# Diagonal bonus terms of the attention: eight scaled ACT copies instead of one POOL multiplication

## The chip, the cores and the metric

The kernel runs on one core of a Trainium2 chip. It is one launch that does an attention with a decaying state, a gated feed-forward block and a mixture of eight experts. The metric is the device time of the core in microseconds (us), lower is better; it is measured in several runs, and one further execution is recorded by the hardware profiler. Engines: TensorE (PE, with its weight loads PEld), VectorE (DVE), ScalarE (ACT), GpSimd (POOL), and SyncE (SP), which issues the DMA transfers.

## The reference, cut to what matters

The attention goes through 768 steps for 4 batches and 8 heads of 48 channels. The part that the change touches is the term with `u`, a bonus for the current step: summed over the channels it is the scalar `sum_d r*k*u` of a head and a position, which multiplies that position's `v`.

```python
for t in range(S):
    kt, vt, rt, wt = (k[:, :, t], v[:, :, t], r[:, :, t], w[:, :, t])
    cur = np.einsum('bhd,bhe->bhde', u[None] * kt, vt)
    y[:, :, t] = np.einsum('bhd,bhde->bhe', rt, state + cur)
    state = wt[:, :, :, None] * state + np.einsum('bhd,bhe->bhde', kt, vt)
...
a = x @ w1; b = x @ w2; h = a * b @ w3; x = h @ w_out
```

Behind it come a gate that is normalised eight times over rows and columns, and eight experts of the form `max(x @ w1[e], 0) @ w2[e]`.

## The kernel before

The attention is done in 24 units of 128 positions (four batches, six units each), all eight heads of a unit together. A unit goes through four phases, one in each step of a loop over steps `s`; the unit is `s // 4`, the phase `s % 4`:

- phase 0: `stage_a0` of the next unit. PE transposes the decays into `trw` and the keys into `trk`; ACT copies `trw` out (L278, tile `w33`, shown as `w<-trw`). Then f_rk multiplies r, k and u on POOL (L305, L306, tile `rk`). Somewhat later in the same step `stage_a1` has PE transpose r into `trr`.
- phase 1: `stage_b`: PE makes the scores `sc`, ACT copies out the transposed keys (`kn`), DVE masks the scores into `A` (L376) and adds the diagonal terms `ec` to it (L377).
- phases 2 and 3: `stage_c1` and `stage_c2`: PE multiplies `A` with the values (`yt`), DVE updates the states, ACT copies the result into `xraw` (L436, L438).

`stage_a0` also queues eight small operations, of which two are taken in each step: two scans on DVE (L309, L312), small products, the scaled keys and r (`Kt`, `Rt`, DVE and POOL) and, as the last, `f_cc`, so that f_cc is reached in phase 3, ahead of the next step's `stage_a0`. f_cc sums `rk` over the channels on DVE (tile `cc`, 128 positions x 8 heads, L344), and makes from it the diagonal terms `ec` (128 x 2 x 4 x 64, L345).

```python
pw = ps.tile([P, NP, P], F32, tag="tr", bufs=2, name="trw")
...
pk = ps.tile([P, NP, P], F32, tag="tr", bufs=2, name="trk")
...
pr = ps.tile([P, NP, P], F32, tag="tr", bufs=2, name="trr")
...
aux.extend([f_scan_f, f_scan_g, f_small, f_ks, f_rp, f_kx, f_rx, f_cc])
```

The three transposes share a PSUM tag with two buffers. The order of each engine's work is the order in which the program emits it; nothing reorders it.

The feed-forward block runs in the same steps, for blocks of three units. From s = 15 on the steps repeat in twelves: eight MoE steps (`moe_a`: nine matmuls into `pa`, ACT copies them to `asb`, L475; `moe_b`: nine into `pb`, DVE multiplies with `asb` to `gs`, L488, ACT rounds to `gh`, L489, POOL keeps the rest `gl`, L490) and four x2 steps (18 matmuls into `po`, ACT copies them out, L518). In an MoE step of phase 0 the order is `stage_a0`, `moe_a`, one queued operation, `stage_a1`, `moe_b`, one queued operation. In the first 30 steps the weights are also unpacked from 64-bit numbers (`cv`, `wo`: ACT L160, DVE L165 to L167; `w1h`, `w2h` ACT L213; `w1l`, `w2l` POOL L214), and a product of two weight matrices is made (`w34`).

After the attention, from about 530 us on, PE works through the experts (`zp`, `yp`).

Of the kernel before, what the change touches and what calls it, by code (L numbers as in the profile page):

```python
# [14 lines left out]
AF = mybir.ActivationFunctionType  # L15
ALU = mybir.AluOpType
# [15 lines left out]
def tile_rwkv_moe_sinkhorn_moe(  # L32
# [16 lines left out]
    nc = tc.nc  # L49
    B, H, S, D = r.shape  # L50
# [3 lines left out]
    P = 128  # L54
    DP = 64
    NP = H // 2
# [18 lines left out]
    def mm(o, lhsT, rhs, start, stop, pos=None, tr=False, skip=False):  # L75
        kw = {}
        if skip:
            kw["skip_group_check"] = True
        if pos is not None:
            kw["tile_position"] = pos  # L80
        if tr:
            kw["is_transpose"] = True
        nc.tensor.matmul(o, lhsT, rhs, start=start, stop=stop, **kw)  # L83
# [4 lines left out]
    eye = const.tile([P, DP], F32, name="eye")  # L88
# [184 lines left out]
    def stage_a0(n):  # L273
        wt, kt = nat["w", n % 2], nat["k", n % 2]
        pw = ps.tile([P, NP, P], F32, tag="tr", bufs=2, name="trw")
        for p in range(NP):
            mm(pw[:, p, :], wt[:, 2 * p:2 * p + 2, :].rearrange("p a d -> p (a d)"), ident, True, True, tr=True)
        nc.scalar.activation(W33B[:, :, 0:32], pw.rearrange("p a (b s) -> p (a b) s", s=32), AF.Copy)  # L278
        pk = ps.tile([P, NP, P], F32, tag="tr", bufs=2, name="trk")
        for p in range(NP):  # L280
            mm(pk[:, p, :], kt[:, 2 * p:2 * p + 2, :].rearrange("p a d -> p (a d)"), ident, True, True, tr=True)
        d = st[n] = {"pk": pk}
        Ft = att.tile([P, 528], F32, tag="F", name="Ft")
        Gt = att.tile([P, 529], F32, tag="G", name="Gt")
        M = att.tile([P, 2, 2, 8], F32, tag="M", bufs=2, name="Mt")
        T12 = att.tile([P, NP, 2], F32, tag="T12", bufs=2, name="T12")
        Rt = att.tile([P, 34 * 32], F32, tag="R", bufs=2, name="Rt")
        rk = att.tile([P, H, D], F32, tag="rk", name="rk")
        cc = att.tile([P, H], F32, tag="cc", bufs=2, name="cc")
        d.update(R=Rt, T12=T12, v=nat["v", n % 2])  # L290
        F3 = Ft.rearrange("p (b s) -> p b s", s=33)
        Fv = F3.rearrange("p (c b) s -> p b c s", b=2)[:, :, :, 0:32]
        Tv = F3.rearrange("p (c b) s -> p b c s", b=2)[:, :, :, 32]
        Gv = Gt[:, 1:529].rearrange("p (c b s) -> p b c s", b=2, s=33)[:, :, :, 1:33]

        def diag(t):
            return t.rearrange("p (g a s) -> p g a s", g=2, s=32)[:, :, 0:16:2, :]

        def off(t):
            return t[:, 32:32 * 31].rearrange("p (g a s) -> p g a s", g=2, s=32)[:, :, 0:15:2, :]  # L300

        nrt, nkt = nat["r", n % 2], nat["k", n % 2]

        def f_rk():
            nc.gpsimd.tensor_tensor(rk, nrt[:, :, 0:D], nkt[:, :, 0:D], op=ALU.mult)  # L305
            nc.gpsimd.tensor_tensor(rk, rk, ub, op=ALU.mult)  # L306

        def f_scan_f():
            nc.vector.tensor_tensor_scan(Ft, w33[:, 0:528], d1[:, 0:528], 0.0, op0=ALU.mult, op1=ALU.add)  # L309

        def f_scan_g():
            nc.vector.tensor_tensor_scan(Gt[:, 2:529][:, ::-1], w33[:, 2:529][:, ::-1], d1[:, 2:529][:, ::-1],  # L312
                                         0.0, op0=ALU.mult, op1=ALU.add)

        def f_small():
            nc.vector.tensor_copy(M[:, :, 1, :], Tv)
            nc.vector.reciprocal(M[:, :, 0, :], M[:, :, 1, :])
            nc.vector.tensor_tensor(T12.rearrange("p a b -> p (a b)"), M[:, 0, 1, :], M[:, 1, 1, :], op=ALU.mult)

        def f_ks():  # L320
            Kt = att.tile([P, 34 * 32], F32, tag="K", bufs=1, name="Kt")
            d["K"] = Kt
            kv = pk.rearrange("p a (c b s) -> p b (a c) s", b=2, s=32)
            nc.vector.tensor_tensor(diag(Kt), kv, Gv, op=ALU.mult)

        def f_kx():
            Kt = d["K"]
            m_ = M[:, 1, :, :].unsqueeze(3).to_broadcast([P, 2, 8, 32])
            for g in range(2):
                nc.gpsimd.tensor_tensor(off(Kt)[:, g], diag(Kt)[:, 1 - g], m_[:, g], op=ALU.mult)  # L330

        def f_rp():
            rv = d["pr"].rearrange("p a (c b s) -> p b (a c) s", b=2, s=32)
            nc.vector.tensor_tensor(off(Rt)[:, ::-1], rv, Fv, op=ALU.mult)

        def f_rx():
            m_ = M[:, 0, :, :].unsqueeze(3).to_broadcast([P, 2, 8, 32])
            for g in range(2):
                nc.gpsimd.tensor_tensor(diag(Rt)[:, g], off(Rt)[:, 1 - g], m_[:, g], op=ALU.mult)

        def f_cc():
            ec = att.tile([P, 2, NP, DP], F32, tag="ec", bufs=1, name="ec")
            d["ec"] = ec
            nc.vector.tensor_reduce(cc, rk, axis=AX.X, op=ALU.add)  # L344
            nc.gpsimd.tensor_tensor(  # L345
                ec, eye.unsqueeze(1).unsqueeze(1).to_broadcast([P, 2, NP, DP]),
                cc.rearrange("p (a h) -> p h a", h=2).unsqueeze(3).to_broadcast([P, 2, NP, DP]), op=ALU.mult)

        f_rk()
        aux.extend([f_scan_f, f_scan_g, f_small, f_ks, f_rp, f_kx, f_rx, f_cc])  # L350
# [725 lines left out]
```

## Time and profile before

| what | value |
|---|---|
| median of 3 runs | 2104.77 us (2103.47 to 2104.82) |
| profiled execution, its own time | 2102.65 us |
| span of its instructions | 2100.9 us |
| mean granted clock of PE | 0.991 |
| PE busy | 2045.1 us |
| DVE, ACT, POOL busy | 1143.0, 552.4, 489.2 us |

The span goes from the first instruction to the last; the rest of the execution's time lies around it. Busy time leaves out waiting. The granted clock is the share of full speed (2.4 GHz) that PE had.

### The profile page before, as it was taken

To read this page: it belongs to the slowest core of one execution; us is meant where nothing else is said; L and a number is where in the kernel's file an instruction comes from. 1 tells how busy PE (TensorE), PEld (TensorE's weight loads), DVE (VectorE), ACT (ScalarE), POOL (GpSimd) and SP (SyncE) were. 2 spreads that over 40 slices of the span, in tenths; PEclk is the share of its full clock that TensorE was granted. 3 is DMA by queue.
4 is the path that set the end of the run, shared out by engine and by line. 5 is a ranking of instruction groups with operands and counts; after the bars stand their busy time and mean duration, and the time that the engine had idled before them with its cause. 6 is when DMAs were issued, how large, how long until landed. Compare 5 with 4: busy or idle time off the path is not lost.

```text
span 2100.9 us, 37959 instructions
## 1 busy us (share of the span) xinstructions
PE 2045.1 (97%) x16427; PEld 1991.1 (95%) x16427; DVE 1143.0 (54%) x1792; ACT 552.4 (26%) x956; POOL 489.2 (23%) x487
## 2 busy tenths in 40 slices
PE   5879999999999999999999999999999999999999
PEld 4569999999999999999999999999999999999999
DVE  8786666661575464454455545544545454445444
ACT  3443333333322221231123112211321131123111
POOL 4475555555513210030003001200300030011000
PEclk8999999999999999999999999999999999999999
DMA  7652222211412222132124122321321232213220
GB/s 229 134 102 49 50 50 50 49 25 48 180 46 91 104 93 91 56 128 104 46 91 146 50 91 69 128 91 46 135 98 54 91 111 86 91 61 117 100 86 31
DMA packets 145287, 183.67 MB, mean 87 GB/s; under 512 B 105120, under 2 KB 133856, under 8 KB 137952
## 3 DMA queue, kind: packets, MB, share of 16 engines
q1 hardware_dynamic: 145120, 181.25, 26.9%
q8 instruction: 129, 2.11, 0.4%
q14 instruction: 38, 0.31, 0.1%
HBM read 161.17 MB, written 18.87 MB: 86 GB/s over the span
## 4 chain that ended last, share of the span: by engine, by line
PE 92%; DVE 4%; DMA 1%; issue 1%; POOL 1%; ACT 1%; SPq 0%; DVEq 0%; ACTq 0%; POOLq 0%
PE yp L83 38%; PE zp L83 35%; PE po L83 5%; PE pa L83 5%; PE pb L83 4%; PE yt L83 1%; DVE cv L166 1%; DMA nat_w<-in_w_dram 1%; PE sc L83 1%; PE trn L83 1%; PE w34ps L83 1%; DVE cv L167 0%; PE trw L83 0%; PE up L83 0%; PE trk L83 0%
## 5 line engine op out<-in xcount | busy, mean ns | idle before, releaser
L83 PE MATMUL zp<-xc,w1h 128*128 128x256 f32 x4224 | 783.2, 280 | 7.7 <-DVE hl L848 6.7
L83 PEld LDWEIGHTS zp<-xc,w1h 128*128 128x128 f32 x4224 | 692.1, 189 | 9.5 <-issue 7.8
L83 PE MATMUL zp<-xc,w1l 128*128 128x256 f32 x2112 | 594.8, 282 | 0.0
L83 PE MATMUL yp<-w2h,hh 128*128 128x384 f32 x1536 | 517.6, 337 | 0.0
L83 PE MATMUL yp<-w2l,hh 128*128 128x384 f32 x1536 | 516.5, 336 | 0.1
L83 PE MATMUL yp<-w2h,hl 128*128 128x384 f32 x1536 | 516.2, 336 | 0.0
L83 PEld LDWEIGHTS zp<-xc,w1l 128*128 128x128 f32 x2112 | 398.7, 189 | 0.0
L844 ACT ACTIVATE hh<-cc 128x512 fp32r<-128x512 f32 x288 | 182.2, 633 | 814.5 <-DVE cc L851 814.5
L652 POOL TENSOR_TENSOR w1l<-w1raw,w1h 128x768 fp32r<-128x768 f32 x32 | 59.2, 1850 | 1086.1 <-ACT w1h L651 1086.1
L83 PEld LDWEIGHTS yp<-w2h,hh 128*128 128x128 f32 x1536 | 289.8, 189 | 0.1
L83 PEld LDWEIGHTS yp<-w2l,hh 128*128 128x128 f32 x1536 | 288.9, 188 | 0.4 <-DVE w2l L666 0.4
L83 PEld LDWEIGHTS yp<-w2h,hl 128*128 128x128 f32 x1536 | 288.4, 188 | 0.0
L851 DVE TENSOR_TENSOR cc<-u,zp 128x512 f32<-128x512 f32 x192 | 131.9, 687 | 270.5 <-PE zp L83 270.5
L851 DVE TENSOR_TENSOR u<-t,zp 128x512 f32<-128x512 f32 x192 | 131.9, 687 | 193.7 <-PE zp L83 162.8
L848 DVE SCALAR_TENSOR_TENSOR hl<-cc,hh 128x512 fp32r<-128x512 f32 x288 | 199.0, 691 | 7.6 <-ACT hh L844 7.4
L959 DVE SCALAR_TENSOR_TENSOR acc<-yp,Pm,acc 128x384 f32<-128x384 f32 x168 | 103.4, 616 | 117.0 <-PE yp L83 116.8
L844 ACT ACTIVATE hh<-zp 128x512 fp32r<-128x512 f32 x96 | 57.5, 599 | 253.0 <-PE zp L83 253.0
L848 DVE SCALAR_TENSOR_TENSOR hl<-zp,hh 128x512 fp32r<-128x512 f32 x96 | 65.8, 686 | 72.8 <-ACT hh L844 72.8
L490 POOL TENSOR_TENSOR gl<-gs,gh 128x384 fp32r<-128x384 f32 x64 | 72.1, 1127 | 109.2 <-ACT gh L489 109.1
L851 DVE TENSOR_TENSOR vv<-u,zp 128x512 f32<-128x512 f32 x96 | 66.1, 688 | 49.2 <-PE zp L83 48.4
L488 DVE TENSOR_TENSOR gs<-pb,asb 128x384 f32<-128x384 f32 x64 | 35.5, 555 | 103.1 <-PE pb L83 65.0
L867 ACT ACTIVATE t<-zp 128x512 f32<-128x512 f32 x96 | 57.4, 598 | 124.4 <-PE zp L83 124.4
(151 smaller groups left out, 2370.3 us busy)
## 6 DMA issues: line engine op xcount, KB each, us to landing
xc<-xd SPq DMA_DIRECT2D x42, 2304.0 KB, 8.7
xd<-xc SPq DMA_DIRECT2D x6, 2304.0 KB, 7.0
w2raw<-in_moe_w_dram SPq DMA_DIRECT2D x32, 384.0 KB, 3.5
raw<-in_moe_w_dram SPq DMA_DIRECT2D x8, 1024.0 KB, 5.0
w1raw<-in_moe_w_dram SPq DMA_DIRECT2D x32, 256.0 KB, 2.8
nat_w<-in_w_dram SPq DMA_DIRECT2D x24, 192.0 KB, 3.7
nat_k<-in_k_dram SPq DMA_DIRECT2D x24, 192.0 KB, 3.5
nat_r<-in_r_dram SPq DMA_DIRECT2D x24, 192.0 KB, 3.7
```

The costliest lines, as they stand in the source:

```text
L83: nc.tensor.matmul(o, lhsT, rhs, start=start, stop=stop, **kw)
L166: nc.vector.scalar_tensor_tensor(cu, lw, 29, cu, op0=ALU.logical_shift_right, op1=ALU.bitwise_or)
L488: nc.vector.tensor_tensor(gs, pb, asb, op=ALU.mult)
L490: nc.gpsimd.tensor_tensor(gl[:, f, :], gs, gh[:, f, :].bitcast(F32), op=ALU.subtract)
L652: nc.gpsimd.tensor_tensor(lo[:, d0:d0 + n, :], src, hi[:, d0:d0 + n, :].bitcast(F32), op=ALU.subtract)
L844: nc.scalar.activation(hh, src, AF.Relu)
L848: nc.vector.scalar_tensor_tensor(hl, src, 0.0, hh.bitcast(F32), op0=ALU.max, op1=ALU.subtract)
L851: nc.vector.tensor_tensor(o, a, b_, op=ALU.add)
L867: nc.scalar.activation(t1, b1, AF.Copy)
L959: nc.vector.scalar_tensor_tensor(dst, ya[t], Pm[:, tt, e:e + 1], dst, op0=ALU.mult, op1=ALU.add)
```

## The change

The sum on DVE stays. Instead of one POOL multiplication of the identity (repeated over the heads) with the sums (repeated over the columns), ACT copies the 128x64 identity once for each head, with that head's sums as a scale per partition, into that head's part of `ec`. The eight copies are emitted at the place where the POOL operation was.

```diff
             nc.vector.tensor_reduce(cc, rk, axis=AX.X, op=ALU.add)
-            nc.gpsimd.tensor_tensor(
-                ec, eye.unsqueeze(1).unsqueeze(1).to_broadcast([P, 2, NP, DP]),
-                cc.rearrange("p (a h) -> p h a", h=2).unsqueeze(3).to_broadcast([P, 2, NP, DP]), op=ALU.mult)
+            for h in range(H):
+                nc.scalar.activation(ec[:, h % 2, h // 2, :], eye, AF.Copy, scale=cc[:, h:h + 1])
```

## Rows read from the trace of the kernel before

**Rows 1.** Busy time by stretch: stretch, length, engines, PEclk, DMA share, GB/s.
```profile
0.00:100.00 100.00, 67.95 (x597) 45.43 (x598) 81.38 (x107) 38.11 (x60) 48.11 (x47) 0.88 0.72 187
100.00:200.00 100.00, 87.55 (x1003) 76.25 (x1002) 76.38 (x108) 37.15 (x71) 63.91 (x50) 0.95 0.44 79
...
400.00:500.00 100.00, 100.00 (x1195) 94.38 (x1194) 50.94 (x92) 33.49 (x74) 50.96 (x52) 1.00 0.17 42
```

**Rows 2.** Tile ec: duration in ns (min/median/max), first and last start.
```profile
L345 POOL TENSOR_TENSOR ec<-eye,cc x24: 1049/1885/2027, 13.4 to 468.7; 128x512 f32<-128x512 f32 x24
```

**Rows 3.** The chain that ended last, at 151 us: start, length, what.
```profile
151.19 1.72 POOL ec L345
...
156.52 2.72 POOL w2l L214
```

**Rows 4.** Timeline around 159 us, DVE and PE: start, length, [idle before].
```profile
158.38 1.40 DVE L377 TENSOR_TENSOR At<-At,ec 128x512 f32<-128x512 f32 x1
...
159.29 0.44 PE L83 MATMUL pb<-xh,w2l 128*128 128x384 f32 x1 [2.05 <-POOL w2l L214]
...
160.71 0.69 PE L83 MATMUL yt<-At,nat_v 64*64 64x64 f32 x32
```

**Rows 5.** Timeline of DVE and POOL in the first 60 us.
```profile
37.53 2.03 POOL L345 TENSOR_TENSOR ec<-eye,cc 128x512 f32<-128x512 f32 x1
38.68 1.95 DVE L167 SCALAR_TENSOR_TENSOR cv<-raw,cv 128x1024 uint32<-128x1024 uint32 x1
...
59.81 1.52 DVE L167 SCALAR_TENSOR_TENSOR cv<-raw,cv 128x1024 uint32<-128x1024 uint32 x1
```

**Rows 6.** ACT's groups by form: busy us, mean ns of one; Pm: ns.
```profile
L489 ACT ACTIVATE gh<-gs 128x384 fp32r<-128x384 f32 x64 | 33.6, 525 | 113.9 <-DVE gs L488 113.9
L213 ACT ACTIVATE w1h<-cv 128x768 fp32r<-128x768 f32 x4 | 3.4, 842 | 11.8 <-DVE cv L167 11.8
L990 ACT ACTIVATE Pm<-L,nmx x1: 444/444/444, 563.4 to 563.4; 128x192 f32<-128x192 f32 x1
```

**Rows 7.** Timeline of ACT and PE in an x2 step of phase 0.
```profile
427.92 0.53 ACT L489 ACTIVATE gh<-gs 128x384 fp32r<-128x384 f32 x1 [1.70 <-DVE gs L488]
428.35 0.36 ACT L436 ACTIVATE xraw<-yt 128x256 f32<-128x256 f32 x1
428.74 0.78 ACT L438 ACTIVATE xraw<-yt 64x256 f32<-64x256 f32 x2
431.62 0.60 ACT L278 ACTIVATE w<-trw 128x512 f32<-128x512 f32 x1 [2.09 <-PE trw L83]
...
434.98 0.60 PE L83 MATMUL trr<-ident,nat_r 128*128 128x128 f32 x4
```

**Rows 8.** Who waited for line L278 (ACT's w): us, times.
```profile
PEld trr L83: 0.8, 3
```

**Rows 9.** Timeline, MoE step of phase 0, first kind, and ACT's w at 449.50.
```profile
396.49 0.54 DVE L344 TENSOR_REDUCE cc<-rk 128x8 f32<-128x384 f32 x1
397.10 0.58 ACT L278 ACTIVATE w<-trw 128x512 f32<-128x512 f32 x1
398.19 0.60 PE L83 MATMUL trr<-ident,nat_r 128*128 128x128 f32 x4
...
449.50 0.58 ACT L278 ACTIVATE w<-trw 128x512 f32<-128x512 f32 x1
```

**Rows 10.** Timeline of an MoE step of phase 0, second kind.
```profile
415.14 0.58 ACT L278 ACTIVATE w<-trw 128x512 f32<-128x512 f32 x1
...
416.26 0.60 PE L83 MATMUL trr<-ident,nat_r 128*128 128x128 f32 x4
```

**Rows 11.** A pause of PE, and busy time with PEclk behind two pauses.
```profile
605.49 0.77 PE L83 MATMUL zp<-xc,w1h 128*128 128x256 f32 x2 [3.26 <-DVE hl L848]
...
159.20:164.00 4.80, 4.71 (x84) 4.40 (x85) 4.52 (x11) 0.79 (x2) 2.64 (x3) 1.00 0.20 40
605.40:610.00 4.60, 4.51 (x24) 4.55 (x25) 2.38 (x4) 0.63 (x1) 0.00 (x0) 0.66 0.60 256
```

## The prediction

> **What bounds the kernel now.** I first read the page's engine totals: TensorE (PE) is busy nearly all the span, ACT and POOL about a quarter of it. An average over stages says little, so next come the busy times by stretches of 100 us [rows 1]. Two regimes can be seen. In the first 200 us PE is busy for 67.95 and 87.55 of 100 us while DVE has 81.38 and 76.38: here DVE, DMA and hand-offs set the pace. From 200 to 500 us PE is busy for 100.00 of every 100 us at a granted clock of 1.00 (the last of these three stretches stands in the rows): whatever makes PE wait there is added to the end, and what merely unloads another engine gives nothing. The operation that changes runs in both regimes, 24 times from 13.4 to 468.7 us [rows 2].
>
> Then I followed the chain of work that ended last through the places where this operation sits. POOL's ec is on it once, at 151.19 us [rows 3]. In the stretch where PE is full the chain is PE alone.
>
> **What is removed.** 24 POOL operations of 1.885 us (median) [rows 2], some 40 us of POOL time. In the full stretch that is worth nothing. Before it, two things can come back.
>
> First, the link at 151 us. POOL runs ec, the two rk products and then w2l without a pause [rows 3], and PE stands for 2.05 us before 159.29 until w2l is there [rows 4]. Without ec, w2l comes at most 1.72 us sooner (ec's share of the chain). What is late next is the masked sum At, which ends at 158.38 + 1.40 = 159.78 us; PE's yt, now at 160.71, reads it [rows 4] and so can move by 0.9 us only. I take 0.9.
>
> Second, DVE is slower beside POOL. One pass of the same line and shape took 1.52 us at 59.81 and 1.95 us at 38.68, where ec ran beside it [rows 5]: 0.43 us more. There are six ec before 155 us, so the bound is 6 x 0.43 = 2.6 us. The other bound is nothing, because POOL's next work moves up into the gap and runs beside DVE instead. I take 1.1, rather less than half. The term is -2 us, its bounds 0 and -(1.72 + 2.6) = -4.3 us.
>
> The Trainium skill (GPSIMD Engine Reference, section 8, Key points) says that POOL shares its SBUF interfaces with VectorE and gets in the way of VectorE instructions with two SBUF inputs. The slower pass agrees; by that rule alone the change would be a gain.
>
> **What is added: eight ACT copies for each unit.** Each is 128x64 with a scale read per partition. The trace has no such row, so the price is built from neighbours [rows 6]. Plain SBUF copies take 525 ns at 384 columns and 842 ns at 768, so 0.826 ns a column. The one ACT operation that reads a per-partition operand (Pm, a bias) takes 444 ns at 192 columns; 128 columns fewer make 444 - 106 = 338 ns. Neighbouring ACT operations overlap: gh starts at 427.92 and lasts 0.53, and the next starts at 428.35 [rows 7], 0.10 us before gh's end. So the copies follow each other every 0.24 us, and eight delay what stands behind them by 1.92 us. Lower bound: the per-partition operand costs nothing, 525 - 320 x 0.826 = 261 ns, less 100, makes 0.16 us, 1.28 for eight. Upper bound: no overlap, 0.338 us, 2.70 for eight. I take the middle, because Pm is the only row with such an operand and overlap shows between other copies.
>
> The Trainium skill (ScalarE: Activation LUTs, section What ACT_TABLE_LOAD costs) gives an ACTIVATE a fixed 186 ns, 0.833 ns a column, 93 ns more for each pointer operand, and an overlap of 93 ns between neighbours. It speaks against splitting one operation into eight, as most of the time is then the fixed part: estimated by it, the eight take 8 x 239 = 1.91 us. No run here shows the eight themselves yet.
>
> **Who stands behind them.** ACT works in order. f_cc is the last of the eight queued operations of a unit and is reached in phase 3, behind gh; next in ACT's program is the evacuation w<-trw of the following step's stage_a0. For that wait DVE's scan and, in PE's program, the transposes trr: the tag "tr" has two buffers, trw and trk hold them, and trr takes trw's, so PE can't write it before ACT has read it. That this wait is real the trace shows: PE's weight load for trr sat idle for ACT's w three times [rows 8].
>
> *MoE steps of the first kind* [rows 9]: cc is ready at 397.03; w starts at 397.10 and ends at 397.68; trr starts at 398.19. The slack is 0.51 us, of which I leave 0.1 to the hand-off: 0.41. With eight copies between gh and w, w ends at 399.60 and trr starts at about 399.70. PE stands for 1.92 - 0.41 = 1.51 us.
>
> *MoE steps of the second kind* [rows 10]: w from 415.14 to 415.72, trr at 416.26. The slack is 0.54, less 0.1, and cc is ready only when ACT comes free, which costs 0.03 more: again 0.41.
>
> *x2 steps* [rows 7]: ACT ends the xraw copies at 429.52 and then waits 2.09 us for trw. Eight copies end at 431.44, before w's start at 431.62, and trr comes only at 434.98. No loss, not even at 2.70 us.
>
> How often: f_cc falls in steps s = 3, 7, ..., 91, and a stage_a0 follows all but the last. From s = 15 on the steps repeat in twelves: two f_cc in MoE steps, one in x2 steps. From 186 us to the end of the attention these are six of the first kind (w every 52.4 us, from 449.50 - 5 x 52.4 = 187.5 to 449.50) and five of the second (from 415.14 - 4 x 52.4 = 205.5 to 415.14): 11. The loss is 11 x 1.51 = 16.6 us; by the bounds 11 x (1.28 - 0.41) = 9.6 and 11 x (2.70 - 0.41) = 25.2.
>
> Behind the stall: the scan starts 1.92 us later and PE 1.51, so DVE is 0.4 us later against PE; gs waits for pb, 2 us after trr, and the scan is over by then. The asb copy moves behind w, and gs needs it only with pb. No DMA is issued by these instructions or moved past a queue. Before 186 us I count no loss: PE is idle 32 and 12 us of 100 there [rows 1], and at 149 us the stall falls into waits that PE has anyway.
>
> **Sum.** -2 + 16.6 = +14.6 us. The profiled execution took 2102.65 us, 2.1 less than the median of the runs, 2104.77; carried over to the median, the forecast is 2119.4 us. The bounds, 9.6 - 4.3 = +5.3 and +25.2, make 2110 and 2130. What a measurement of this kernel can tell from no change is about 0.2%, 4 us.
>
> **Rivals.** *The clock falls.* The stalls could bring PE to its lower level, 1.2 GHz, for a while. For: before 605.49 PE idled 3.26 us, and the stretch behind it had a mean granted clock of 0.66. Against: behind the stop of 2.05 us before 159.29 it stayed at 1.00 [rows 4, 11], and the stalls I expect are shorter. Price: (1 - 0.66) x 4.6 = 1.6 us each, 17 in all: 2137 us.
>
> *The relief wins (the other side).* POOL's time in the first 190 us would have to come back whole. Seven ec there make at most 7 x 1.885 = 13.2 us [rows 2]; against the smallest loss, 9.6, that gives 2101 us. It decides only where the relief exceeds the stalls. Against it: the chain has POOL's ec once [rows 3], and PE is full afterwards.
>
> *The copies hide.* If eight take less than 0.41 us (51 ns each, about the column time alone), or trr turns out not to wait for w, the change only frees POOL: 2104.77 - 2 = 2102.8 us. Against: each ACT row has a fixed part of about 0.2 us [rows 6], and the wait is in the trace [rows 8].
>
> **How the numbers follow.** Forecast 0.82, clock 0.06, relief 0.05, hidden 0.07. The first two are slower: 0.88. The relief is faster with 0.02 and same with 0.03; the hidden copies are within 0.2% with 0.05 and, with the largest relief, faster with 0.02. So faster 0.04, same 0.08, slower 0.88. The range is the forecast's, 2110 to 2130.
>
> **What would show it.** In the profile after: eight ACT copies of 128x64 within about 2 us between gh and w; PE waiting at trr for ACT's w, some 1.5 us in eleven MoE steps and not in x2 steps; a cycle of about 55.4 instead of 52.4 us; a clock of 1.00 throughout it; the time from the end of the attention on unchanged. The forecast is wrong if the copies follow each other much faster than 0.24 us, if the clock falls, or if the first 190 us shrink by more than 5 us.

## The result and the profile after

The median is 2117.57 us (2115.25 to 2119.35) against 2104.07 us for the kernel before in runs on the same chips: +13.5 us, a ratio of 1.0065, 95% interval 1.0055 to 1.0075. The change makes the kernel slower. The forecast was +14.6 us.

The profiled execution took 2118.07 us, its span is 2116.1 us (before 2100.9, so 15.2 longer). First the busy time by stretch (same columns as [rows 1]):

```profile
100.00:200.00 100.00, 87.29 (x1032) 76.36 (x1031) 72.73 (x108) 44.79 (x103) 54.26 (x44) 0.95 0.44 80
...
400.00:500.00 100.00, 96.12 (x1172) 89.70 (x1172) 50.49 (x93) 41.62 (x112) 37.11 (x42) 1.00 0.14 30
```

PE, which was full from 200 us on, now has gaps of 4 to 5 us in each 100 there, at a granted clock of 1.00. POOL has less to do and ACT more; neither is anywhere near full. What the new ACT copies are, from the view of the tile ec (duration in ns, first and last start):

```profile
L346 ACT ACTIVATE ec<-eye,cc x192: 331/333/350, 11.8 to 482.7; 128x64 f32<-128x64 f32 x192
```

Their order in an MoE step of the first kind, the answer to [rows 9], is in the timelines of ACT and PE (x8 are eight instructions drawn together; the bracket gives the idle time before and what ended it):

```profile
405.55 0.53 ACT L488 ACTIVATE gh<-gs 128x384 fp32r<-128x384 f32 x1 [1.79 <-DVE gs L487]
405.98 2.01 ACT L346 ACTIVATE ec<-eye,cc 128x64 f32<-128x64 f32 x8
407.89 0.57 ACT L278 ACTIVATE w<-trw 128x512 f32<-128x512 f32 x1
...
406.89 0.34 PE L83 MATMUL pa<-xh,w1l 128*128 128x384 f32 x1
408.52 0.66 PE L83 MATMUL trr<-ident,nat_r 128*128 128x128 f32 x4 [1.29 <-ACT w L278]
...
463.33 0.57 ACT L278 ACTIVATE w<-trw 128x512 f32<-128x512 f32 x1
```

The eight start at 405.98 and w at 407.89: w is late by 1.91 us, 0.239 a copy. PE stands at trr until w ends (408.46). The last row is the same place one cycle (twelve steps) later: a cycle now takes 55.44 us where it took 52.4. The second kind, the answer to [rows 10], shows the same:

```profile
427.49 0.57 ACT L278 ACTIVATE w<-trw 128x512 f32<-128x512 f32 x1
...
428.11 0.66 PE L83 MATMUL trr<-ident,nat_r 128*128 128x128 f32 x4 [1.30 <-ACT w L278]
```

and an x2 step, the answer to [rows 7], shows the copies in ACT's idle time, with no wait at trr:

```profile
440.65 0.78 ACT L437 ACTIVATE xraw<-yt 64x256 f32<-64x256 f32 x2
441.46 2.02 ACT L346 ACTIVATE ec<-eye,cc 128x64 f32<-128x64 f32 x8
443.53 0.60 ACT L278 ACTIVATE w<-trw 128x512 f32<-128x512 f32 x1
...
446.89 0.60 PE L83 MATMUL trr<-ident,nat_r 128*128 128x128 f32 x4
```

Who waited for ACT's w (us in total, times), the answer to [rows 8], where PE's weight loads for trr had 0.8 us in three waits:

```profile
PEld trr L83: 21.2, 15
PE trr L83: 16.0, 12
```

Eleven of PE's twelve waits lie behind 186 us, 1.29 or 1.30 us idle each; the twelfth is at 150 us:

```profile
150.02 0.65 PE L83 MATMUL trr<-ident,nat_r 128*128 128x128 f32 x4 [1.78 <-ACT w L278]
```

The idle 1.29 us in the bracket is less than what a wait costs: two waits lengthen a cycle by 55.44 - 52.40 = 3.04 us, so one costs 1.52 us. In the kernel before, trr does not let the last matmul into pa run out:

```profile
398.01 0.34 PE L83 MATMUL pa<-xh,w1l 128*128 128x384 f32 x1
```

There trr starts at 398.19 [rows 9], 0.16 us ahead of that matmul's end; after the wait this overlap is missing, and the four transposes take 0.66 instead of 0.60 us. 1.29 + 0.16 + 0.06 makes 1.51 us.

The account of the profiled execution: PE reaches trw of the first of the eleven waits at 182.93 us (before 186.15), so 3.2 us were gained up to there; 11 x 1.52 = 16.7 us are lost from there on; in the chain of work that ended last, PE's expert matmuls (zp) begin at 543.64 instead of 530.16 us, +13.5. The other 1.7 us of the span arise in the expert phase, 1.5 of them between two pauses of PE (582.27 to 620.55 us here, 568.74 to 605.49 before), where PE's clock fell behind the first pause in this execution and did not in that of before:

```profile
582.27 0.47 PE L83 MATMUL zp<-xc,w1h 128*128 128x256 f32 x2 [2.26 <-DVE hl L847]
...
584.00:590.00 6.00, 6.00 (x36) 6.00 (x36) 2.63 (x7) 1.26 (x2) 0.00 (x0) 0.78 0.23 98
```

The same place in the kernel before:

```profile
568.74 0.48 PE L83 MATMUL zp<-xc,w1h 128*128 128x256 f32 x2 [2.26 <-DVE hl L848]
...
570.50:576.50 6.00, 6.00 (x43) 6.00 (x42) 3.97 (x12) 1.26 (x2) 0.00 (x0) 1.00 0.23 98
```

The pause is 2.26 us in both; the mean granted clock behind it is 0.78 here and 1.00 there. In the profiled executions of the seven kernels below, two of which keep POOL's operation whole, the clock fell behind this pause each time, so the kernel before is the exception. I take it for scatter between executions: one profile of a kernel can't show that, but the mean granted clock over whole runs of the kernel before goes from 0.986 to 0.993. The medians differ by the 13.5 us of the attention.

### The profile page after: what moved, and what is told of

Same layout as the page of the kernel before. It is cut to its first block, busy times and chain, and to the rows that moved or that the text cites. A ratio compares the mean times of both kernels' runs of the same rounds, so it can differ in the third digit from the quotient of the medians.

```text
span 2116.1 us, 38125 instructions
## 1 busy us (share of the span) xinstructions
PE 2049.1 (97%) x16427; PEld 1991.6 (94%) x16427; DVE 1129.6 (53%) x1792; ACT 597.4 (28%) x1148; POOL 437.9 (21%) x463
## 4 chain that ended last, share of the span: by engine, by line
PE 90%; DVE 5%; ACT 2%; DMA 1%; issue 1%; POOL 1%; SPq 0%; DVEq 0%; ACTq 0%
PE yp L83 38%; PE zp L83 35%; PE po L83 5%; PE pb L83 4%; PE pa L83 3%; ACT ec L346 1%; PE yt L83 1%; DVE cv L166 1%; PE sc L83 1%; DMA nat_w<-in_w_dram 1%; PE trr L83 1%; DVE cv L167 1%; PE trn L83 1%; DVE gs L487 1%; ACT gh L488 0%
```

## The experiments

The theory: PE stands at trr, because ACT reaches w late by the time of eight copies. Rival 1: ACT's added work costs wherever it stands. Rival 2: DVE's later scan is what costs. The table has all seven runs; "trw" is when PE starts the transposes of the first of the eleven MoE steps behind 186 us, "cycle" the distance of trw in two successive cycles.

| kernel | ratio to before (95%) | trw, us | cycle, us |
|---|---|---|---|
| before | 1 | 186.15 | 52.40 |
| changed | 1.0065 (1.0055 to 1.0075) | 182.93 | 55.44 |
| copies behind w | 0.9986 (0.9977 to 0.9995) | 182.39 | 52.40 |
| trr behind pb | 0.9986 (0.9977 to 0.9995) | 182.87 | 52.41 |
| copies beside POOL, one place | 1.0160 (1.0146 to 1.0174) | 185.74 | 57.4 to 59.0 |
| neither copies nor POOL | 0.9990 (0.9981 to 0.9999) | 184.65 | 52.40 |
| copies, then POOL | 1.0076 (1.0062 to 1.0090) | 185.25 | 55.49 |
| half of the heads on ACT | 1.0025 (1.0015 to 1.0035) | 184.68 | 53.60 |
| POOL in the eleven | 0.9985 (0.9976 to 0.9994) | 182.54 | 52.40 |

**Copies behind w.** Only the order of the copies and of w on ACT is exchanged.

```diff
-            for h in range(H):
-                nc.scalar.activation(ec[:, h % 2, h // 2, :], eye, AF.Copy, scale=cc[:, h:h + 1])
+            ecq.append(f_ec)          # f_ec holds these two lines
...
         nc.scalar.activation(W33B[:, :, 0:32], pw.rearrange("p a (b s) -> p (a b) s", s=32), AF.Copy)
+        if ecq:
+            ecq.popleft()()
```

> The same eight ACT copies, emitted behind ACT's copy w<-trw of the next step instead of in front of it; nothing else changes. Theory (PE stands at trr because w is late by the time of eight copies): the eleven waits at trr are gone, the cycle of three units is back at 52.4 us, and what is left is the relief of the first 190 us: some 2.4 us under the kernel before, ratio 0.9988. Rival 1 (ACT's added work as such delays what it hands over, wherever it stands): as the changed kernel, ratio 1.0065. Rival 2 (the later start of DVE's scan is what costs): gone as well, since the scan starts in time again; the run with trr moved tells that apart.

Measured: 2101.2 us, ratio 0.9986. ACT and PE in the step that answers to the one at 405 us:

```profile
393.35 0.58 ACT L279 ACTIVATE w<-trw 128x512 f32<-128x512 f32 x1
393.82 2.01 ACT L351 ACTIVATE ec<-eye,cc 128x64 f32<-128x64 f32 x8
395.74 0.47 ACT L481 ACTIVATE asb<-pa 128x384 f32<-128x384 f32 x1
...
394.43 0.60 PE L83 MATMUL trr<-ident,nat_r 128*128 128x128 f32 x4
```

ACT does the same work in the same step, and asb is as late as in the changed kernel (3.75 us behind the start of trw here, 3.74 in the changed kernel, 2.69 in the kernel before); trr has no wait. Rival 1 falls. This version is below both kernels.

**trr behind pb.** The changed kernel, with PE's order changed instead of ACT's.

```diff
-            if n < NU - 1 and ph == 0:
-                stage_a1(n + 1)
             moe_b(sl[1], sl[2], asb)
+            if n < NU - 1 and ph == 0:
+                stage_a1(n + 1)
             pop(1)
```

> The changed kernel with its eight copies in front of w, but in MoE steps of phase 0 the transposes trr are emitted behind the nine matmuls into pb instead of in front of them. Theory: PE reaches trr some 1.57 us later, so the slack is 0.39 + 1.57 = 1.96 us against a delay of w of 1.91: the waits at trr all but vanish, cycle 52.4 to 52.6 us, ratio about 0.999. Rival 2 (late scan): w and the scan start as late as in the changed kernel, so the cycle stays near 55.4 us and the ratio at 1.0065. Rival 1: the same as rival 2.

Measured: 2100.9 us, ratio 0.9986.

```profile
393.87 2.01 ACT L346 ACTIVATE ec<-eye,cc 128x64 f32<-128x64 f32 x8
395.79 0.58 ACT L278 ACTIVATE w<-trw 128x512 f32<-128x512 f32 x1
...
396.52 0.60 PE L83 MATMUL trr<-ident,nat_r 128*128 128x128 f32 x4
```

w is as late behind gh as in the changed kernel and DVE's scan with it (3.87 us behind the start of trw in both), but PE now comes to trr after w's end (396.37). The loss is gone with w still late, so rival 2 falls too: it is the wait at trr alone.

**Copies beside POOL, into one place.** The cost without the relief.

```diff
             nc.gpsimd.tensor_tensor(ec, ...)      # as before
+            for h in range(H):
+                nc.scalar.activation(junk, eye, AF.Copy, scale=cc[:, h:h + 1])
```

> The kernel before with its POOL operation kept, and eight ACT copies of the same form in front of w, into a tile that nobody reads. It has the cost alone. Theory: 11 waits of 1.52 us and no relief, +16.7 us, ratio 1.0079, with the first 190 us as in the kernel before. If the relief of the changed kernel came from something else than POOL's freed time (for instance from how transfers fell in that run), this run shows the early part shorter too, ratio near 1.0065.

Measured: ratio 1.0160, twice the expected loss; the expectation missed. Two things differ from the changed kernel, both in the trace (ACT and PE of one step, then the stretch of PE behind it, then a pause of the same length in a step of the second kind and the stretch behind that):

```profile
418.19 3.00 ACT L350 ACTIVATE junk<-eye,cc 128x64 f32<-128x64 f32 x8
421.09 0.58 ACT L279 ACTIVATE w<-trw 128x512 f32<-128x512 f32 x1
...
421.72 1.09 PE L83 MATMUL trr<-ident,nat_r 128*128 128x128 f32 x4 [2.28 <-ACT w L279]
...
421.70:424.00 2.30, 2.28 (x9) 2.28 (x10) 1.82 (x1) 0.35 (x1) 0.71 (x1) 0.52 0.00 0
...
384.90 0.66 PE L83 MATMUL trr<-ident,nat_r 128*128 128x128 f32 x4 [2.30 <-ACT w L279]
...
384.90:387.50 2.60, 2.60 (x41) 2.35 (x45) 1.99 (x2) 0.33 (x1) 0.64 (x1) 1.00 0.00 0
```

Copies that all write the same place follow each other every (421.09 - 418.19) / 8 = 0.36 us instead of 0.239, so w is 2.90 us late and a wait costs 2.5 us (57.4 instead of 52.4 us for a cycle of two waits in which the clock does not fall). And behind two of the eleven pauses, this one and one at 248 us, PE's granted clock fell to about half, the lower level of 1.2 GHz, for some 3.5 us; that cycle is 1.4 to 1.6 us longer, near the 1.6 us that the prediction had as the price of a fall. Behind the others, the one at 384.90 among them, it stayed at 1.00. So the rival "the clock falls" is real at pauses of 2.3 us, where the changed kernel has 1.3.

**Neither copies nor POOL.** The relief without the cost.

```diff
-            nc.gpsimd.tensor_tensor(ec, ...)
+            d["ec"] = ec0                          # zeros, made once
```

> The kernel before without the POOL operation and without copies: DVE adds a tile of zeros made once, so the bonus term of the attention is left out. It has the relief alone. Theory: only the first 190 us shorten, by 1.7 to 2.5 us (DVE passes beside POOL, 0.9 to 1.6, and the link of w2l at 151 us, 0.8); cycle 52.4 us as before; ratio 0.9988 to 0.9992. Rival: POOL's time is worth nothing anywhere, ratio 1.000.

Measured: 2101.96 us, ratio 0.9990, 2.2 us under the kernel before; the cycle is that of before, and in the profiled execution the attention's first part is 1.5 us shorter. So POOL's time is worth something, but only before 186 us, and about 0.1%.

**Copies, then POOL.** The cost alone, with copies that overlap.

```diff
+            for h in range(H):
+                nc.scalar.activation(ec[:, h % 2, h // 2, :], eye, AF.Copy, scale=cc[:, h:h + 1])
             nc.gpsimd.tensor_tensor(ec, ...)      # as before
```

> The cost alone once more, with copies that overlap as in the changed kernel: eight ACT copies into the eight places of ec, and then the POOL operation of the kernel before writes the same ec. (In the run with one spare tile each copy waited for the one before it, and eight took 2.9 us.) Theory: w late by 1.91 us in eleven MoE steps, 11 x 1.52 = 16.7 us and no relief: ratio 1.0079, cycle 55.4 us. If the granted clock falls behind pauses of 1.3 us too, the cycle is longer than that by some 1.4 us each time.

Measured: ratio 1.0076, +16 us, and a cycle of 55.49 us. One of the waits:

```profile
189.14 0.66 PE L83 MATMUL trr<-ident,nat_r 128*128 128x128 f32 x4 [1.29 <-ACT w L278]
```

The clock stayed at 1.00 behind all eleven waits, of 1.29 to 1.36 us. This is the number that the one-place run should have given.

**Half of the heads on ACT.**

```diff
-            for h in range(H):
+            for h in range(H // 2):
                 nc.scalar.activation(ec[:, h % 2, h // 2, :], eye, AF.Copy, scale=cc[:, h:h + 1])
+            nc.gpsimd.tensor_tensor(ec[:, :, 2:, :], ...)      # heads 4 to 7
```

> The changed kernel with four heads copied by ACT and the other four made by one POOL operation of half the size. Theory: w late by 4 x 0.239 = 0.96 us, slack 0.39, so 0.57 us in each of eleven steps, 6.2 us, less about half of the relief (1.2): +5 us, ratio 1.0024, cycle 52.4 + 2 x 0.57 = 53.5 us. Rival (each visit of the copies costs the same, whatever their number): near the changed kernel, 1.0065.

Measured: ratio 1.0025, cycle 53.60 us, 0.60 us a wait, of which PE is idle for 0.33 to 0.41:

```profile
187.62 0.66 PE L83 MATMUL trr<-ident,nat_r 128*128 128x128 f32 x4 [0.33 <-ACT w L278]
```

The loss goes with the delay of w less the slack, not with the visit: w late by 0.96, 1.91 and 2.90 us (the last in the one-place run) costs 0.60, 1.52 and 2.5 us a wait.

**POOL in the eleven.**

```diff
+            if n <= 5 or n % 3 == 0:
+                ...                                 # eight ACT copies
+            else:
+                nc.gpsimd.tensor_tensor(ec, ...)
```

> The changed kernel with POOL's operation put back for the eleven units whose copies come in MoE steps after 186 us, and for the last unit; ACT copies for the first six units and for those of the x2 steps. Theory: the copies cost nothing where ACT idles or PE waits anyway; cycle 52.4 us, what remains is the relief of the first 190 us: ratio 0.9988, like the run with the copies behind w. Rival 1 (ACT's added work costs anywhere): 13 of 24 sets of copies remain, so about half of the loss, ratio 1.003.

Measured: 2101.37 us, ratio 0.9985. Twelve of the 24 sets of copies remain in this kernel, not thirteen as the expectation has it. At the first of the eleven places trr no longer waits:

```profile
184.98 0.60 PE L83 MATMUL trr<-ident,nat_r 128*128 128x128 f32 x4
```

Copies that fall into ACT's idle time, or into the part where PE waits anyway, cost nothing; the whole loss is in the eleven places.

## Why the prediction was right, point by point

*The price of the copies* held: 0.239 us from copy to copy (forecast 0.24), 333 ns for one (338). The Pm row was the right neighbour, and the overlap of neighbouring copies held, as long as they write different places. Estimated by the figures of the Trainium skill (ScalarE: Activation LUTs, section What ACT_TABLE_LOAD costs), the copies follow each other every 239 ns, and the trace agrees with its 0.239 us.

*Who waits* held and is shown from three sides: with w back in front of the copies, with trr moved behind w's end, and with the copies out of the eleven steps, the cycle is back at 52.4 us each time. The wait of 1.51 us was measured as 1.52, the cycle of 55.4 as 55.44. That it fits to 0.01 us is luck: the hand-off took 0.06 us and not 0.1, and the 0.06 by which the transposes then take longer was not counted. The dose is right as well: 0.57 expected with four copies, 0.60 measured.

*Eleven places, none in x2 steps* held (runs with POOL in the eleven and the changed kernel's own trace).

*The relief* is the term that the runs support least. Forecast -2 us with bounds 0 and -4.3; the profiled execution shows -3.2. Not all of that is POOL's freed time: the run that has the relief alone shows 1.5 us in its trace and 2.2 by medians, and the two kernels that keep POOL's work whole and add copies reach trw at 185.74 and 185.25 us, 0.4 to 0.9 before the kernel before. The traces can be divided at the trw of the MoE step ahead of the link, at 147.79 us in the kernel before. From there to the trw of the table it takes 38.36 us before, and 37.53 to 37.58 us in the five kernels that take the POOL operation out of that part: 0.8 us, the link, in every one of them. With all or half of the POOL operation kept it is 38.5 to 39.5. Up to 147.79 us the gain is 2.4 to 3.0 us in the five kernels where copies stand in for all or half of POOL's operation there, 1.1 in the two that keep it whole beside copies, and only 0.7 in the one without either. So what the changed kernel gained above the link is not explained by POOL's time alone, and that the forecast for it (1.1 us, chosen between two bounds) is of the right order is partly luck.

Part of the gain is at the two places named. The DVE pass beside POOL and the link, after:

```profile
36.40 1.99 POOL L305 TENSOR_TENSOR rk<-nat_r,nat_k 128x384 f32<-128x384 f32 x1
37.55 1.92 DVE L167 SCALAR_TENSOR_TENSOR cv<-raw,cv 128x1024 uint32<-128x1024 uint32 x1
42.87 1.23 DVE L167 SCALAR_TENSOR_TENSOR cv<-raw,cv 128x1024 uint32<-128x1024 uint32 x1
...
152.21 2.69 POOL L214 TENSOR_TENSOR w2l<-cv,w2h 128x768 fp32r<-128x768 f32 x1
...
156.69 0.69 DVE L376 TENSOR_TENSOR At<-At,ec 128x512 f32<-128x512 f32 x1
...
157.49 0.69 PE L83 MATMUL yt<-At,nat_v 64*64 64x64 f32 x32 [0.91 <-issue]
```

The answer to [rows 5] is the expected one: POOL's rk moved up into ec's place and the pass at 37.55 is as slow as it was beside ec (1.92 against 1.95); the gain comes some passes later, when POOL has run out of work: the pass at 42.87 takes 1.23, where it took 1.91 in the kernel before:

```profile
44.03 1.91 DVE L167 SCALAR_TENSOR_TENSOR cv<-raw,cv 128x1024 uint32<-128x1024 uint32 x1
```

So a pass beside POOL costs 0.68 us more and not the 0.43 of the prediction: its pass of 1.52 us at 59.81 was no free one, as POOL's work on Rt (57.70 to 60.25) ran into it. The answer to [rows 4] is that PE no longer waits for w2l (POOL ends it at 154.90) but, as forecast, for At: yt starts right behind it (At ends at 157.38), 0.9 us after PE was ready; the profile names no releaser for this pause ("issue"), so this is read from the times. It moved from 160.71 to 157.49, 3.2 us, of which 2.4 us had been gained before (PE's yt of the unit before moved from 143.91 to 141.49): 0.8 for the link, forecast 0.9. How the rest divides between DVE and transfers that happened to land earlier can't be told from single traces, and stays open.

*No loss before 186 us* held for the one wait of PE at trr there: PE stood 1.78 us at 150.02 us in the changed kernel, but the way from trw of that step to the trw of the table takes 37.58 us there and 37.56 with the copies behind w, where this wait is missing.

*The rivals.* The clock did not fall behind the eleven waits of the changed kernel, and did at longer pauses in the one-place run. The relief did not win: by medians it is 2.2 to 3.2 us in the four runs without the waits. The copies did not hide.

*Sum.* By medians +13.5 us against +14.6. The loss was sized within 0.1 us, so the relief would be some 1 us too small; but the interval of the ratio goes from +11.6 to +15.8 us, and the times alone don't show that.

## What to carry to other kernels

Whether a copy on an engine with much idle time is free depends on where it stands: look at what is next behind it in that engine's order, who waits for that, and how much slack the wait has now. Here 1.9 us of ACT work in each unit cost 16.7 us in all in front of w and nothing behind it. Where PE was full, unloading POOL gave nothing (a cycle of 52.40 us with its operation and without), and the slack of a buffer shared by two tiles (here the PSUM tag of trw and trr) is the number to compute before moving work.

## What the runs showed of the hardware that had not been expected

Eight ACT copies of 128x64 follow each other every 0.239 us when each writes a place of its own, and every 0.36 us when all write the same place; what holds them apart there was not tried. And a pause of PE of 2.26 to 2.30 us lowers its granted clock in some cases and not in others: at the same place of the expert phase it did behind 2.26 us in the changed kernel (0.78 over the next stretch) and in all seven kernels of the experiments, and did not behind 2.26 us in the kernel before (1.00); and within one execution it did behind two of eleven pauses of 2.3 us.
